# A short list of five slots after batch 3, GpSimd in one fixed order, and dilated values loaded ahead of plain queries

## The chip, the cores and the metric

The kernel runs on one core of a Trainium2 chip. The metric is the device time of one execution in microseconds (us); the time before is a median of 3 runs. A core has engines that run side by side, each in its own order of instructions: TensorE (PE, with its weight loads shown as PEld), VectorE (DVE), ScalarE (ACT), GpSimd (POOL) and SyncE (SP). SP only issues transfers here (16 DMA engines move them), and GpSimd issues some too: plain stores, scatters and gathers by index.

## What is computed

Two stages. The first is banded attention over 8 batches, 8 heads, 576 positions and 64 channels: heads 0 to 3 ("plain") see the last 32 positions, heads 4 to 7 ("dilated") every fourth of the last 128. The second is a mixture of 8 experts with one expert to a token, over the 8 x 576 = 4608 rows of 512 channels that attention gives.

```python
rel = pos[:, None] - pos[None, :]
mask_plain = (rel >= 0) & (rel < window)                                        # window = 32
mask_dil = (rel >= 0) & (rel < window * dilation) & (rel % dilation == 0)       # dilation = 4
...
logits = x @ w_gate + modality_bias[modality_id]
e_idx = np.argmax(logits, axis=1)
...
for e in range(E):
    mask = e_idx == e
    ...
    h = np.maximum(x[mask] @ w1[e], 0.0)
    out[mask] = gate_w[mask, None] * (h @ w2[e])
```

The weights of one expert are 512x1024 and 1024x512 floats, 4 MB together. The bias of the modality (spread 0.5) outweighs the rest of the logits, so that nearly all tokens go to few experts. Counted with the reference for its inputs at seed 0, all 4608 tokens split into 1621, 2290 and 697 for experts 1, 6 and 7; those of batches 0 to 3 into 821, 1114 and 369, those of batches 0 to 4 into 1047, 1396 and 437.

## The kernel before, in words

**Units and steps.** Attention goes by units: a batch has nine, `m` = 0 to 8 (L676 to L680): four of plain heads, one mixed (`m` = 4), four of dilated heads, 128 score rows each. The main loop (L942) makes one step `t` for each of the 72 units and overlaps them: step `t` emits the scores of unit `t` (matmuls L340, mask L343, maximum L346, and the subtraction on GpSimd, L347), the exponent of unit `t`-1 on ACT (L351), the transposed probabilities of `t`-2 (L356, L359), the product with the values of `t`-3 (L365, L380), the transposed output of `t`-4 (L387 to L392) with its store to `x_dram` by GpSimd (L402), and the gate's logits of `t`-5 (L411).

**Order.** PE, DVE, ACT and SP run in the order of the program's text (`MANUAL`, L20, L920). GpSimd isn't in that set: calls through `pool` (class `InOrder`, L269) pass `keep_in_program_order` and leave their name in `state['pool']`; the scatters into `table` (L497) are held behind that one instruction, and nothing else ties the calls to each other. L274, the line in `InOrder`, is the profile's line for all of them.

**Loads.** SP issues all loads of a batch in program order: `k` and `q` come in tiles `st` of four heads (L116, 4 transfers of 144 KB), plain values `vw` in one transfer (L127), dilated values in twelve of 16 to 64 KB (L131). For the batch after, dilated `k` is issued at the end of step `m`=1, dilated `q` at `m`=2, plain values at the start of `m`=3; for the batch after that, plain `k` at the end of `m`=6 and plain `q` at `m`=7; the first six transfers of the next batch's dilated values come at the end of `m`=8, and the other six at the start of `m`=0. ACT copies a shifted edge of the values at the end of steps `m` = 0 to 2 (plain) and 4 to 6 (dilated) (`shift_v`, L137). `qk_chunks` turns `k` and `q` on PE in six chunks (L306), two in a step: the next batch's plain ones in `m` = 4 to 6, k first, then q, its dilated ones in `m` = 8, 0 and 1.

**Routing.** Five steps after the last unit of a batch, a task `background` (L719) is made; `advance` runs one piece of each task, twice in a step. `gating` finds each token's expert, rank and weight and scatters (row, weight, number) into `table`, 96 tokens at a time. After the batch named in `EARLY` (batch 4), `slot_info` makes a short list of the full slots of 256 tokens that can be served at once, here three; `fetch_slot` loads the rows' numbers of a slot (`idt`, L626, SP), `gather` fetches the rows (`xr`, four gathers by GpSimd, each followed by two pieces' pause, into one buffer), writes them to `x_slot` (L645, SP) and reads them back as `xg` (L651, SP). After batch 7 the same `slot_info` makes the list of all other slots, in 39 instructions of DVE or so.

**Slots.** There are 19 slots of one expert each: 18 of 256 tokens and a last one of 128. Each is eight rounds `f` of 12 matmuls 128x256 (L858), ReLU and split on ACT and DVE (L864, L865), and 6 matmuls 128x512 (L838); the weights are split into a high and a low part for each slot (L806, L807), two rounds ahead. An expert's 4 MB are loaded only where a slot's expert differs from the one before (L657 to L669). `slots` is a generator (`moe`), started at step 71 (`go` at L755), that the main loop advances between attention's steps by `step`, and after them `while not state['routed']` by one piece for two pieces of the routing (L1017 to L1020).

Of the kernel before, what the change touches and what calls it, by code (L numbers as in the profile page):

```python
# [22 lines left out]
B, H, S, D = 8, 8, 576, 64  # L23
# [12 lines left out]
GB = 96  # L36
NGB = S // GB
SLOT = 256
EARLY = ((4, 3),)
NEARLY = sum(n for _, n in EARLY)  # L40
NSTAT = 18 - NEARLY
NIDS = 6
# [22 lines left out]
def kernel(  # L65
# [73 lines left out]
    state = {('qk', 0, 0): load_qk(0, 0, nc.scalar)}  # L139
# [129 lines left out]
    class InOrder:  # L269


        def __getattr__(self, name):
            def issue(*args, **kw):
                ins = tc.keep_in_program_order(getattr(nc.gpsimd, name)(*args, **kw))  # L274
                state['pool'] = ins.ins
                return ins
            return issue

    pool = InOrder()
# [439 lines left out]
    def background(b):  # L719


        if b < B - 1:
            yield
        steps = gating(b, state['lT', b])
        if b in round_of:
            for _ in steps:
                yield
                if ('counts', b) in state:
                    break
            yield from together(steps, slot_info(state['counts', b], round_of[b]))  # L730
            if round_of[b] > 0:
                return
            yield
            for n in range(2):
                fetch_slot(n)
                yield
            for _ in gather(0, ids_of[0]):
                yield
                yield

            while state['t'] < (B - 1) * 9:
                yield
            for _ in range(3):
                load_more(0, 1)
                yield
                yield
            steps = prepare_x(0, ids_of[0])
            for i in range(6):
                if i % 2 == 0:
                    load_more(0, 1)  # L750
                next(steps, None)
                yield
            while state['t'] < NU - 2:
                yield
            state['go'] = True  # L755
            return
        yield from steps
        if b == B - 1:
            yield
            yield from slot_info(state['counts', b], len(EARLY))  # L760
            yield from rest_info()
            state['routed'] = True

    def run(*pieces):
        for p in pieces:
            for _ in p:
                pass

    def together(*pieces):

        pieces = list(pieces)
        while pieces:
            for p in list(pieces):
                if next(p, pieces) is pieces:
                    pieces.remove(p)
            yield
# [150 lines left out]
    def step(share=MOE_RATE / 6):  # L927

        nonlocal credit
        if moe:  # L930
            credit += share if state['t'] < NU else 1
            while credit >= 1:
                credit -= 1
                next(moe, None)
# [7 lines left out]
    for t in range(NU + LAG + 1):  # L942
# [5 lines left out]
            psum['o'] = ctx.enter_context(tc.tile_pool(name="ps_o1", bufs=1, space=PSUM))  # L948
            moe = slots(NS, ids_of, ahead, hold)
        b, m = t // 9, t % 9  # L950
        if t == 1:
            pieces = qk_chunks(1, *state['qk', 0, 1])
        if t < NU:
            jobs = order[t][1]
            if m == 0:
                state['lT', b] = gwk.tile([2 * NE, S], F32, name="lT")
            if b + 1 < B:
                if m == 4:
                    pieces = qk_chunks(0, *state['qk', b + 1, 0])
                elif m == 8:  # L960
                    pieces = qk_chunks(1, *state['qk', b + 1, 1])
            if m == 0 and b > 0:
                load_v(b, 1, slice(6, None))
            elif m == 3:
                if b + 1 < B:
                    state['v', b + 1, 0] = load_v(b + 1, 0)
            units.append(Unit(b, m, jobs, [state['v', b, 0], state['v', b, 1]] if m >= 4 else [state['v', b, 0]], state['lT', b]))
            units[t].scores()
# [21 lines left out]
            units[t - 4].store()  # L990
            units[t - 4].keep(pool)

        for h in {0: (0,), 1: (1,), 2: (2, 3)}.get(m, ()) if 2 < t < NU else {0: (0, 1), 1: (2, 3)}.get(t, ()):
            shift_v(b, 0, h)
        for h in {4: (0,), 5: (1,), 6: (2, 3)}.get(m, ()) if t < NU else ():
            shift_v(b, 1, h)
        for i in range(2):
            step()
            if i < len(pieces):
                pieces[i]()  # L1000
        pieces = pieces[2:]
        if t < NU and b + 1 < B:

            if m == 1:
                state['k', 1] = load_one(b + 1, 1, k)
            elif m == 2:
                state['qk', b + 1, 1] = load_one(b + 1, 1, q), state['k', 1]
            elif m == 6 and b + 2 < B:
                state['k', 0] = load_one(b + 2, 0, k)
            elif m == 7 and b + 2 < B:  # L1010
                state['qk', b + 2, 0] = load_one(b + 2, 0, q), state['k', 0]
            elif m == 8:
                state['v', b + 1, 1] = load_v(b + 1, 1, slice(0, 6))
        advance([*round_of, B - 1] if moe and t < NU else range(-1, B))


    while not state['routed']:  # L1017
        step(1)
        advance()
        advance()  # L1020
    run(moe)
    man.close()
# [34 lines left out]
```

## Time and profile before

| what | value |
|---|---|
| time before, median of 3 runs | 711.53 us (710.65 to 712.71) |
| profiled execution, its own time | 710.85 us |
| span of the profile (first to last instruction) | 709.1 us |
| mean granted clock of TensorE | 0.959 |
| PE busy | 649.3 us (92%) |
| DVE, ACT, POOL busy | 497.4, 437.9, 290.0 us |
| moved by DMA | 94.95 MB, 134 GB/s |
| SP's queue (q1) | 146612 packets, 63.89 MB |

How to read it: times in the views are us from the span's start. A row of the timeline has start, length, engine, line, operation, what it writes and reads, and in brackets how long the engine had been idle and who ended that. A row of a table by stretches gives the stretch, its length, each engine's busy time with its number of instructions, the granted TensorE clock (1.00 is full, 0.50 half), the DMA engines' busy share and GB/s. SP's rows are issues, not landings.

### The profile page before, as it was taken

Reading aid. Unit: us, or ns where it says so; the run is one execution under the profiler, and the core shown is the slowest. Engines: PE = TensorE matmul, PEld = TensorE weight load, DVE = VectorE, ACT = ScalarE, POOL = GpSimd, SP = SyncE. Lnnn points to the kernel's source line nnn. Section 1 sums busy time; section 2 is a strip of 40 time slices with the busy share of each in tenths; the row PEclk is TensorE's granted clock in tenths of the full one; section 3 lists DMA queues with packets and bytes.
Section 4 is the critical chain, followed back from the end, with each engine's and each line's share of the span. In section 5 each row is a group of like instructions: output and inputs, shape, how many; then the busy total and the mean of one; then the engine's idle time right before and its main releaser. Section 6 shows DMA issues by size and latency. Waiting matters only on the chain. (4 is left out here: it accounts for less than half of the span.)

```text
span 709.1 us, 17888 instructions
## 1 busy us (share of the span) xinstructions
PE 649.3 (92%) x6286; PEld 571.1 (81%) x6286; DVE 497.4 (70%) x1212; ACT 437.9 (62%) x964; POOL 290.0 (41%) x396
## 2 busy tenths in 40 slices
PE   6799998997887899799999999999999999999991
PEld 3688787786776688689999999999999999999980
DVE  1688886886876778677766776667766677667660
ACT  3587896886766656355665565565666556655650
POOL 7345774865668553533333232233313231310110
PEclk7799999999899699999999999999999999999996
DMA  9898698697976943213433972333222346821730
GB/s 159 144 233 180 150 193 169 150 195 145 166 167 159 257 131 77 61 61 91 138 131 78 263 185 79 74 114 106 96 83 82 99 120 182 219 74 46 203 86 13
DMA packets 163233, 94.95 MB, mean 134 GB/s; under 512 B 124144, under 2 KB 143090, under 8 KB 163140
## 3 DMA queue, kind: packets, MB, share of 16 engines
q1 hardware_dynamic: 146612, 63.89, 40.3%
q0 software_dynamic: 11120, 28.64, 13.4%
q10 hardware_dynamic: 5408, 1.24, 1.0%
q8 instruction: 51, 0.84, 0.6%
q14 instruction: 42, 0.34, 0.2%
HBM read 127.52 MB, written 29.39 MB: 221 GB/s over the span
## 5 line engine op out<-in xcount | busy, mean ns | idle before, releaser
L858 PE MATMUL pt<-xh,w1l 128*128 128x256 f32 (+1 forms) x608 | 172.9, 284 | 7.7 <-DVE w1l L807 7.7
L858 PE MATMUL pt<-xl,w1h 128*128 128x256 f32 (+1 forms) x608 | 172.3, 283 | 0.0
L858 PE MATMUL pt<-xh,w1h 128*128 128x256 f32 (+1 forms) x608 | 172.2, 283 | 0.0
L864 ACT ACTIVATE hh<-pt 128x256 fp32r<-128x256 f32 (+1 forms) x152 | 57.6, 379 | 159.5 <-PE pt L858 159.4
L807 DVE TENSOR_TENSOR w2l<-w2q,w2h 128x512 fp32r<-128x512 f32 x152 | 104.9, 690 | 43.0 <-ACT w2h L806 34.7
L274 POOL DMA_INDIRECT xr<-x_dram,idt x74 | 82.5, 1115 | 120.4 <-DMA x_slot<-xr 72.2
L858 PEld LDWEIGHTS pt<-xh,w1l 128*128 128x128 f32 x608 | 116.7, 192 | 8.6 <-DVE w1l L807 8.5
L858 PEld LDWEIGHTS pt<-xh,w1h 128*128 128x128 f32 x608 | 116.5, 192 | 6.8 <-ACT w1h L806 0.2
L858 PEld LDWEIGHTS pt<-xl,w1h 128*128 128x128 f32 x608 | 116.6, 192 | 5.7
L838 PE MATMUL py<-w2h,hh 128*128 128x512 f32 x296 | 118.1, 399 | 0.0
L838 PE MATMUL py<-w2h,hl 128*128 128x512 f32 x296 | 117.1, 396 | 0.0
L838 PE MATMUL py<-w2l,hh 128*128 128x512 f32 x296 | 116.1, 392 | 0.0
L865 DVE SCALAR_TENSOR_TENSOR hl<-pt,hh 128x256 fp32r<-128x256 f32 (+1 forms) x152 | 63.3, 416 | 73.9 <-ACT hh L864 73.8
L274 POOL DMA_INDIRECT out_dram<-ys,idt x37 | 39.6, 1071 | 179.4 <-ACT ys L841 115.8
L807 DVE TENSOR_TENSOR w1l<-w1q,w1h 128x512 fp32r<-128x512 f32 x152 | 104.1, 685 | 2.7 <-ACT w1h L806 2.7
L806 ACT CAST w1h<-w1q 128x512 fp32r<-128x512 f32 x152 | 94.4, 622 | 3.3 <-DMA w1q<-in_moe_w_dram 3.3
L806 ACT CAST w2h<-w2q 128x512 fp32r<-128x512 f32 x152 | 93.1, 612 | 0.0
L274 POOL TENSOR_TENSOR sm<-sm,nmx 128x384 f32<-128x384 f32 x72 | 59.8, 830 | 61.9 <-DVE den L372 45.5
L365 PE MATMUL po<-vw,pT 96*64 96x65 f32 x1152 | 57.0, 238 | 11.3 <-ACT pT L359 6.7
L359 ACT COPY pT<-pt 96x512 f32<-96x512 f32 x72 | 41.5, 576 | 41.3 <-PE pt L356 40.2
L838 PEld LDWEIGHTS py<-w2l,hh 128*128 128x128 f32 x296 | 55.8, 189 | 13.2
L365 PEld LDWEIGHTS po<-vw,pT 96*64 96x64 f32 x1152 | 44.5, 145 | 24.6 <-ACT pT L359 11.4
(160 smaller groups left out, 1110.7 us busy)
## 6 DMA issues: line engine op xcount, KB each, us to landing
w2q<-in_moe_w_dram SPq DMA_DIRECT2D x76, 512.0 KB
w1q<-in_moe_w_dram SPq DMA_DIRECT2D x152, 256.0 KB
st<-in_k_dram SPq DMA_DIRECT2D x64, 144.0 KB
x_slot<-xr SPq DMA_DIRECT2D x18, 512.0 KB
xg<-x_slot SPq DMA_DIRECT2D x72, 128.0 KB
x_dram<-x_sb POOLq DMA_DIRECT2D x32, 256.0 KB, 3.6
st<-in_q_dram SPq DMA_DIRECT2D x56, 144.0 KB
vw<-in_v_dram SPq DMA_DIRECT2D x8, 576.0 KB
```

The lines of the kernel that those rows point to most:

```text
L274: ins = tc.keep_in_program_order(getattr(nc.gpsimd, name)(*args, **kw))
L359: nc.scalar.copy(out=self.pT, in_=src)
L365: nc.tensor.matmul(out=pov[u * TQ:(u + 1) * TQ, h, :], lhsT=self.pT[:, h, u * TQ:(u + 1) * TQ], rhs=self.vts[kd][:, h, i, :], start=True, ...
L806: nc.scalar.copy(out=hi, in_=raw)
L807: nc.vector.tensor_tensor(out=lo, in0=raw, in1=hi.bitcast(F32), op=ALU.subtract)
L838: nc.tensor.matmul(out=py[u], lhsT=ht[:, us], rhs=wt, start=(f + n == 0), stop=(f + n == FC + 1))
L858: nc.tensor.matmul(out=ph, lhsT=wt[:, c, :], rhs=xt[:, c, 0:cols], start=(c + i == 0), stop=(c + i == KC + 1))
L864: nc.scalar.activation(out=hh, in_=ph, func=AF.Relu)
L865: nc.vector.scalar_tensor_tensor(out=hl, in0=ph, scalar=0.0, in1=hh.bitcast(F32), op0=ALU.max, op1=ALU.subtract)
```

## The change

It does five things. The short list is made after batch 3 and has five slots instead of three; its pieces come at half the pace (`spaced`). The gathers of slot 0 come one a step from step 48 on at the earliest, those of slot 1 one a step from step 57 on, before the slots' generator starts, which finds slot 1's rows under way (`fetching`, `todo['rows'] = 2`). Each call through `pool` is placed behind the one before it. The dilated values of the next batch are issued at the ends of `m`=7 and `m`=8, and plain queries after them, at the end of `m`=0; at the kernel's start the turning of dilated q and k and the edge copies move by a step. After the last step the routing gets one piece for three pieces of the slots, not two for one.

```diff
-EARLY = ((4, 3),)
+EARLY = ((3, 5),)
...
                 ins = tc.keep_in_program_order(getattr(nc.gpsimd, name)(*args, **kw))
+                if 'pool' in state:
+                    tc.add_manual_dep(ins.ins, state['pool'].name, mybir.DependencyInfo(mybir.DependencyClass.NoSync, mybir.DependencyReason.SCHED_ONLY),
+                                      reason="GpSimd's order")
                 state['pool'] = ins.ins
...
-            yield from together(steps, slot_info(state['counts', b], round_of[b]))
+            yield from together(steps, spaced(slot_info(state['counts', b], round_of[b])))
...
-            for _ in gather(0, ids_of[0]):
-                yield
-                yield
+
+            for n, t0 in ((0, (b + 1) * 9 + 12), (1, (b + 2) * 9 + 12)):
+                rows = gather(n, ids_of[n])
+                while state['t'] < t0:
+                    yield
+                for _ in range(4):
+                    next(rows)
+                    yield
+                    yield
+                if n == 0:
+                    for _ in rows:
+                        yield
+            fetching.append((1, rows))
+            todo['rows'] = 2
...
+    def spaced(piece):
+
+        for _ in piece:
+            yield
+            yield
...
-        if t == 1:
+        if t == 2:
             pieces = qk_chunks(1, *state['qk', 0, 1])
...
-            if m == 0 and b > 0:
-                load_v(b, 1, slice(6, None))
-            elif m == 3:
+            if m == 3:
...
-        for h in {0: (0,), 1: (1,), 2: (2, 3)}.get(m, ()) if 2 < t < NU else {0: (0, 1), 1: (2, 3)}.get(t, ()):
+        for h in {0: (0,), 1: (1,), 2: (2, 3)}.get(m, ()) if 2 < t < NU else {1: (0, 1), 2: (2, 3)}.get(t, ()):
             shift_v(b, 0, h)
...
-        for i in range(2):
-            step()
+        at_once = 3 if t < 4 else 2
+        for i in range(at_once):
+            if i < 2:
+                step()
             if i < len(pieces):
                 pieces[i]()
-        pieces = pieces[2:]
+        pieces = pieces[at_once:]
...
-            elif m == 7 and b + 2 < B:
-                state['qk', b + 2, 0] = load_one(b + 2, 0, q), state['k', 0]
+            elif m == 7:
+                state['v', b + 1, 1] = load_v(b + 1, 1, slice(0, 6))
             elif m == 8:
-                state['v', b + 1, 1] = load_v(b + 1, 1, slice(0, 6))
+                load_v(b + 1, 1, slice(6, None))
+            elif m == 0 and b > 0:
+                state['qk', b + 1, 0] = load_one(b + 1, 0, q), state['k', 0]
...
     while not state['routed']:
-        step(1)
-        advance()
+        for _ in range(3):
+            step(1)
         advance()
```

## The prediction

> **What bounds the kernel now.** I read the page first, then tables by stretches, then waits, then timelines of single engines. The page's first line and a table of engines by stretch give the frame. The first seven stretches are the batches 1 to 7; the eighth is the first two slots with attention's last units among them; the last is the other 17 slots.
>
> ```profile
> span 709.1 us, 17888 instructions
> ...
> core 0: us, PE busy (x) PEld busy (x) DVE busy (x) ACT busy (x) POOL busy (x), PEclk, DMA share, GB/s
> 44.20:70.60 26.40, 24.75 (x445) 21.24 (x443) 22.40 (x75) 22.19 (x55) 13.48 (x24) 1.00 0.85 188
> 70.60:97.10 26.50, 24.91 (x445) 21.30 (x443) 22.60 (x75) 22.12 (x55) 19.01 (x30) 1.00 0.80 169
> 97.10:127.10 30.00, 26.49 (x446) 22.59 (x443) 22.70 (x76) 22.32 (x55) 18.99 (x30) 0.94 0.88 174
> 127.10:154.10 27.00, 25.10 (x445) 21.25 (x443) 22.53 (x75) 22.11 (x55) 18.89 (x30) 1.00 0.85 175
> 154.10:185.70 31.60, 26.85 (x453) 22.85 (x450) 23.10 (x79) 22.28 (x55) 19.00 (x30) 0.95 0.87 163
> 185.70:217.80 32.10, 27.46 (x446) 22.98 (x443) 25.68 (x93) 22.55 (x55) 22.51 (x33) 0.95 0.66 149
> 217.80:252.20 34.40, 28.01 (x406) 23.20 (x405) 24.72 (x79) 21.19 (x51) 23.17 (x33) 0.75 0.90 220
> 252.20:312.10 59.90, 52.55 (x393) 46.38 (x391) 46.26 (x134) 30.11 (x66) 29.11 (x30) 0.97 0.27 73
> 312.10:693.30 381.20, 380.76 (x2438) 344.82 (x2436) 267.19 (x470) 228.31 (x473) 101.61 (x92) 1.00 0.42 120
> ```
>
> I set the stretches so that each batch holds its 9 units x 16 = 144 score matmuls; the same table for line 340 alone shows it for the last:
>
> ```profile
> 217.80:252.20 34.40, 6.26 (x144) 4.25 (x144) 0.75 0.90 220
> ```
>
> Batches 1 and 2 take 26.4 and 26.5 us (mean 26.45) at full clock, with PE, DVE and ACT all above 80% busy: that is the pace where nothing waits. Batches 3 to 7 are over it by 3.5, 0.5, 5.1, 5.6 and 7.9 us, 22.6 together. In the 17 slots PE is never free (380.8 of 381.2 us); nothing there can be won by order. One slot, from a stretch of exactly eight rounds, is the first row here; the others are the stretches in which the clock was halved, and one with an expert's load in it:
>
> ```profile
> 334.80:357.35 22.55, 22.55 (x145) 20.46 (x144) 16.02 (x29) 13.60 (x29) 6.89 (x6) 1.00 0.37 118
> 117.92:121.33 3.41, 3.41 (x37) 3.07 (x30) 2.73 (x9) 3.06 (x9) 0.82 (x1) 0.50 1.29 242
> 193.02:196.43 3.41, 3.41 (x39) 2.96 (x39) 2.67 (x10) 2.88 (x8) 2.45 (x4) 0.50 0.35 77
> 227.15:237.39 10.24, 9.40 (x105) 7.80 (x106) 7.09 (x19) 7.52 (x18) 8.72 (x10) 0.50 1.06 251
> 302.25:305.65 3.40, 3.11 (x12) 2.97 (x13) 3.22 (x9) 1.19 (x3) 0.00 (x0) 0.50 0.04 2
> 400.00:420.00 20.00, 20.00 (x129) 18.05 (x128) 13.56 (x26) 12.09 (x25) 6.64 (x7) 1.00 0.73 198
> ```
>
> Two slots are 45.1 us, so of the stretch of 59.9 us 14.8 are attention's tail and waits. The waits that ended before the halved stretches, in PE's and ACT's timelines and PE's waits from 292 to 303 us:
>
> ```profile
> 116.71 0.55 PE L306 MATMUL pt<-ident,st 96*128 96x96 f32 x4 [2.35 <-ACT kT L311]
> ...
> 173.60 0.62 ACT L137 COPY vw<-vw 32x520 f32<-32x520 f32 x1 [4.83 <-DMA st<-in_k_dram]
> ...
> 192.49 0.24 PE L411 MATMUL po<-uxl,wgs 128*16 128x128 f32 x1 [1.85 <-DVE uxl L392]
> ...
> 227.99 1.14 PE L365 MATMUL po<-vw,pT 96*64 96x65 f32 x16 [3.30 <-ACT pT L359]
> ...
> PE pt L858 <- DVE w1l L807: 6.3, 2, 5.2
> ```
>
> So: batches 3 and 5 wait for dilated values (ACT stands at the edge copy; the releaser's name is the queue's, the tile copied is `vw`), batch 6 for DVE, batch 7 for the probabilities, the slots for the split weights.
>
> **The change, part by part.**
>
> *Dilated values ahead of plain queries.* SP's issues in batches 4 and 5, and PE where it meets the queries in unit (5, 4):
>
> ```profile
> 128.50 9.19 SPq L131 DMA_DIRECT2D vw<-in_v_dram  x12
> ...
> 152.40 4.07 SPq L116 DMA_DIRECT2D st<-in_q_dram  x4
> 156.57 14.14 SPq L131 DMA_DIRECT2D vw<-in_v_dram  x12
> ...
> 176.63 0.58 SPq L127 DMA_DIRECT2D vw<-in_v_dram  x1
> ...
> 161.89 0.56 PE L340 MATMUL pss<-kT,qT 64*64 64x96 f32 x16
> ...
> 168.21 0.49 PE L306 MATMUL po<-ident,st 96*128 96x96 f32 x4
> ...
> 169.20 0.56 PE L340 MATMUL pss<-kT,qT 64*64 64x96 f32 x16
> ```
>
> Queries took 4.07 us to issue, the twelve value transfers 14.14 (9.19 a batch before). Swapped, values come 4.07 us sooner, and ACT's 4.83 us of waiting fall to about 0.8. But the queries then end where the values ended, at 170.7, and PE wants them in the same step, at 168.21. Chunk 0 takes heads 0 and 1, the first two of four transfers, half of 4.07 or 2 us before the last; with about 2 us from issue to landing (170.7 to 173.6 was 2.9) PE would stand from 168.2 to about 171 or 172. It stood 3.27 us before, some instructions further on. The wait moves more than it goes. Batch 3 alike: PE's 2.35 us become about 2. I take -0.5 us for batches 3 and 4 together, between -3.5 (all of batch 3's excess) and +1. In batch 5 the short list's six scatters now run one every half step beside batch 4's end, not beside the values; if the transfers' 14.14 us fall towards 9.19, the queries come in time. I take a PE wait of 2 us there, not 4.
>
> *At the start*, dilated k and q are turned a step later. The plain queries of batch 1 come by the same loads as before, none of which the edit moves, and unit 5 stands behind them either way; what is won ahead of them is waited away. 0 us, at worst a halved window more, 1.7.
>
> *List after batch 3, gathers spread, GpSimd in order.* GpSimd from 199 to 230 us, SP's load of row numbers, and PE's largest wait from 200 to 213:
>
> ```profile
> 201.53 0.39 SPq L626 DMA_DIRECT2D idt<-table  x1
> ...
> 204.83 1.09 POOL L274 DMA_INDIRECT xr<-x_dram,idt  x1 [3.81 <-DMA idt<-table]
> ...
> 222.34 1.08 POOL L274 DMA_INDIRECT xr<-x_dram,idt  x1 [0.30 <-DVE uxl L392]
> 223.72 1.02 POOL L274 DMA_INDIRECT xr<-x_dram,idt  x1 [0.30 <-DVE den L373]
> 225.05 1.00 POOL L274 DMA_INDIRECT xr<-x_dram,idt  x1 [0.30 <-issue]
> 226.07 0.84 POOL L274 TENSOR_TENSOR sm<-sm,nmx 128x384 f32<-128x384 f32 x1
> ...
> PE po L365 <- ACT pT L359: 0.8, 1, 0.8
> ```
>
> At 222 us three gathers of slot 1 run in a row ahead of unit 65's subtraction; in the program's text they come only after step 71. That is batch 7's wait of 3.30 us, after which the clock was halved for 10.24 us. With the order fixed and these gathers at steps 57 to 60, one a step, both should go. Batch 7 goes from 34.4 to 28: -6.5 us. Not all 7.9, since it carries slot 0's preparation; between -7.9 and -3 (if the clock stays low for other reasons).
>
> Batch 6 loses the list's instructions (93 against 75 of DVE: 18, and 3.1 us more busy than in batch 2), PE's 1.85 us with a halved window behind it, slot 0's gathers and their 3.81 us for row numbers. It gets slot 1's four gathers (about 1.05 us and 0.3 idle each, 5.4 us of GpSimd, which is busy 22.5 of 32.1), and SP's write and read-back of slot 0. Slot 1's first gather needs the one buffer that this write empties, and the write stands behind batch 7's plain queries. -3 us, between -5.6 and 0.
>
> Batch 5 gets the list, at half pace, and slot 0's gathers. Here is the price. The row numbers are issued in step 49, behind the plain values of batch 6; those were due at step 48 (161.89) and were issued at 176.63, for SP runs 14.7 us behind its text in the full batches. The numbers would go out near 177.5, and from issue to gather it took 3.3 us in the row above (201.53 to 204.83) with little ahead of them; behind 576 KB some 2 more. The gather can run at 181 to 183, and stands on GpSimd right after unit 50's subtraction, at 169.2 + 2 (the queries) + 3 (my estimate from the scores to the end of the subtraction): 174 or so. GpSimd then waits 7 to 9 us, and the next subtraction behind it. A wait of 3.81 us cost PE 0.8 at most, so PE pays about 8 - 3.8 = 4 us, and 1.7 for a halved window. Batch 5: 26.45 + 2 + 4 + 1.7 less what overlaps, against 31.6; I say 33.6, +2 us, between -5 (row numbers early enough, no wait for queries) and +7.
>
> *Routing spread over the slots.* DVE from 294 to 301.25:
>
> ```profile
> 294.00:301.25 7.25, 6.42 (x40) 1.00 0.04 2
> ```
>
> The list of the other slots, 37 small instructions, fills DVE in one block while PE waits 6.3 us for split weights; then 3.4 us at half clock, of which half is lost: 8.0 us. After the change one piece comes for three of the slots' pieces: 11 pieces over 33, at four to a round eight rounds of 22.55/8 = 2.8 us. A slot leaves DVE 22.55 - 16.0 = 6.5 us idle and the splits run two rounds ahead, so about 6 us of list fit. Five slots, 113 us, cover it instead of three. -7.5 us, between -8 and -3.
>
> *Two more loads of an expert.* Full slots after batch 3, from the reference: 3 + 4 + 1 = 8, so five exist: three of expert 1 and two of expert 6; then 1 and 6 come again, two loads of 4 MB more. From 400 to 420 us such a load ran at 198 GB/s and PE was busy 20.00 of 20. A load takes 21 us of a slot's 22.55: 0 us, at worst +2.
>
> Sum: -0.5 + 2 - 3 - 6.5 - 7.5 = -15.5 us. The profiled execution took 710.85, 0.7 below the median of 711.53, so 696.0 against the median.
>
> **A rule of the clock.** Waits of 2.35 and 1.85 us were each followed by 3.41 us at 0.50 in the rows above, so I charge a halved window (1.7 us where PE is full) even to short waits. [...]
>
> **The rivals.**
>
> *Waits stay hidden.* SP catches up with the values moved (scatters out of their way): batch 5 ends 4 us under before and batch 6 5 us: -23.5, 688 us. For it: batch 6's wait of 3.81 us cost almost nothing. Against: SP's 14.7 us. 15%.
>
> *Attention wins nothing.* It is held by SP's queue, and what batch 7 gains, batches 5 and 6 lose; only routing's 7.5 remain: 704 us. 17%.
>
> *Slower: GpSimd in order becomes the bound.* A gather that waits for a transfer now holds every later subtraction and routing step. The waits of gathers on slot writes in all of before:
>
> ```profile
> POOL xr L274 <- DMA x_slot<-xr: 72.2, 14, 12.2
> ```
>
> If row numbers take 10 us and the buffer of slots 1 and 2 the longest, 12.2, each above a cover of 3.8: 6.2 + 8.4 + 8.4 = 23 us, with three halved windows 28, of which 5.7 are in my sum: +22, 718 us. It decides from GpSimd waits of about 27 us in all. For it: the order is strict and SP late; against: two gathers have a step between. 9%.
>
> [...] 4%.
>
> *It does not do what it says*, or gains and waits cancel: an empty slot in the list would cost 22.55 us, which the counts exclude; 711 us, 5%.
>
> **How the numbers follow.** My forecast has the other 50%, with its own range of 690 to 702. The range of 686 to 707 takes in most of the first two rivals and leaves out the slower one and the null: about 2 in 10. Faster is 50 + 15 + 17 + 4 = 86%, the same (within 0.3%, 2 us, about what a measurement of this kernel can tell) 5%, slower 9%.
>
> **What would show it.** In the profile after: batch 7 without three gathers in a row and PE without the 3.30 us; no block on DVE and no 5 us wait for `w1l` in the first slots; in batches 3 and 5 PE waiting at `st` (L306's line) for queries in place of ACT at `vw`; a gather in batch 5 with 7 to 9 us of idle time before it, released by `idt`. I am wrong if GpSimd's waits reach PE in the slots, if the last 17 slots show PE idle, or if batches 5 and 6 together take less than 58 or more than 67 us.

## The result and the profile after

The kernel after took 719.82 us (median of 4 runs, 716.37 to 724.02) against 712.12 us (4 runs, 710.65 to 715.17) for the kernel before: a ratio of 1.0102, 95% interval 1.0067 to 1.0136. It is slower, by 1%, where 15.5 us less were forecast. In a second set of runs it was 710.01 us (10 runs) against 706.36 (25 runs), 1.0044 (1.0019 to 1.0069): slower again, by less.

The profiled execution took 717.73 us. Line numbers of the kernel after are 3 above those of before up to the loads (L672), and 20 above them in the slots. First the page's line and the table of engines by stretch, cut at the same work as in the prediction: batches 1 to 7, slots 0 and 1, slots 2 to 18.

```profile
span 715.9 us, 17862 instructions
...
core 0: us, PE busy (x) PEld busy (x) DVE busy (x) ACT busy (x) POOL busy (x), PEclk, DMA share, GB/s
44.00:70.50 26.50, 24.86 (x448) 21.28 (x447) 22.51 (x75) 22.32 (x56) 13.57 (x24) 1.00 0.80 185
70.50:96.90 26.40, 24.85 (x444) 21.21 (x444) 22.58 (x76) 22.28 (x55) 18.97 (x30) 1.00 0.78 167
96.90:126.10 29.20, 26.28 (x444) 22.39 (x443) 22.86 (x76) 22.35 (x55) 18.91 (x30) 0.94 0.81 166
126.10:159.90 33.80, 28.23 (x452) 24.01 (x450) 23.24 (x79) 22.46 (x55) 18.96 (x30) 0.90 0.81 163
159.90:195.30 35.40, 27.52 (x445) 23.06 (x443) 26.55 (x94) 22.73 (x55) 21.49 (x33) 0.90 0.73 151
195.30:227.00 31.70, 25.41 (x445) 21.37 (x443) 24.87 (x81) 23.36 (x57) 27.99 (x39) 1.00 0.91 176
227.00:256.70 29.70, 25.83 (x407) 21.25 (x405) 23.34 (x73) 20.43 (x48) 15.34 (x25) 0.83 0.82 186
256.70:308.70 52.00, 50.88 (x391) 44.96 (x391) 40.49 (x104) 30.24 (x65) 28.39 (x28) 1.00 0.37 107
308.70:699.90 391.20, 384.17 (x2437) 345.74 (x2435) 271.42 (x501) 228.09 (x472) 109.32 (x95) 1.00 0.50 137
```

Two stretches are shorter than before: batch 7 (29.7 for 34.4) and slots 0 and 1 (52.0 for 59.9 us). Batch 4 grew by 6.8, batch 5 by 3.8. The last row has 10.0 us more than before, and PE is no longer busy in all of it: 384.2 of 391.2 us, against 380.8 of 381.2. PE's largest waits, over the whole span, say at what it stood:

```profile
PE po L309 <- DMA st<-in_q_dram: 11.1, 5, 4.2
PE po L475 <- DVE oh L466: 7.7, 7, 4.6
PE pt L878 <- ACT w1h L826: 5.4, 4, 2.5
```

The columns are us in total, times and longest. The first is the wait for plain queries (1.4 us in the kernel before), the second that for the gating, most of it in batch 5, and the third is in the slots, for ACT's split of expert weights. ACT in turn waits for their load, in its own waits of before and of after:

```profile
ACT w1h L806 <- DMA w1q<-in_moe_w_dram: 3.3, 2, 1.8
```

```profile
ACT w1h L826 <- DMA w1q<-in_moe_w_dram: 15.1, 4, 5.0
```

**Batches 4 and 5.** PE's timeline, at one place in each:

```profile
144.53 0.52 PE L309 MATMUL po<-ident,st 96*128 96x96 f32 x4 [4.25 <-DMA st<-in_q_dram]
...
187.95 0.27 PE L475 MATMUL po<-oh,upper 96*96 96x48 bf16 x1 [4.62 <-DVE oh L466]
```

Behind the second stand GpSimd and SP; their timelines (GpSimd's rows first, then SP's, then one of DVE's):

```profile
179.72 0.82 POOL L274 TENSOR_TENSOR sm<-sm,nmx 128x384 f32<-128x384 f32 x1 [2.21 <-DVE den L375]
185.96 1.10 POOL L274 DMA_INDIRECT xr<-x_dram,idt  x1 [5.41 <-DMA idt<-table]
187.09 0.29 POOL L274 TENSOR_TENSOR t<-t,ewt 96x48 f32<-96x48 f32 x1
...
177.59 1.54 SPq L127 DMA_DIRECT2D vw<-in_v_dram  x1
180.52 3.26 SPq L629 DMA_DIRECT2D idt<-table  x2
...
187.42 0.23 DVE L464 TENSOR_REDUCE m<-t 96x6 f32<-96x48 f32 x1 [4.17 <-POOL t L274]
```

Slot 0's first gather stood 5.41 us at the row numbers, which SP issued from 180.5 on. The gating's `t` came only at 187.09, behind the gather; DVE stood 4.17 us at it, and `oh` (DVE, 187.69) and PE's L475 follow from it. GpSimd began `t` 0.03 us after the gather's end.

**The slots.** GpSimd and SP ahead of slot 15, which loads an expert and starts at 610.6:

```profile
586.30 1.45 POOL L274 DMA_INDIRECT xr<-x_dram,idt  x1 [6.85 <-DMA x_slot<-xr]
588.06 1.31 POOL L274 DMA_INDIRECT xr<-x_dram,idt  x1 [0.30 <-issue]
594.18 1.03 POOL L274 DMA_INDIRECT out_dram<-ys,idt  x1 [4.81 <-ACT ys L861]
597.72 1.13 POOL L274 DMA_INDIRECT out_dram<-ys,idt  x1 [2.51 <-ACT w1h L826]
599.15 1.55 POOL L274 DMA_INDIRECT xr<-x_dram,idt  x1 [0.30 <-issue]
601.00 1.01 POOL L274 DMA_INDIRECT xr<-x_dram,idt  x1 [0.31 <-issue]
...
607.88 0.39 SPq L648 DMA_DIRECT2D x_slot<-xr  x1
...
611.00 1.81 SPq L654 DMA_DIRECT2D xg<-x_slot  x4
613.15 2.19 SPq L669 DMA_DIRECT2D w1q<-in_moe_w_dram  x4
```

A slot's four gathers come two ahead of two output scatters and two behind them; the scatters wait for results (4.81 and 2.51 us). So the rows of the slot (`x_slot`) go out 19.8 us after the running slot's start (588.1), and the second half of `w1`, behind them on SP, 2.5 us after slot 15 has begun. In the kernel before the four gathers of slot 15 stand in a row, ahead of the scatters; `x_slot` goes out 12.3 us after the running slot's start at 583.1, and this half of `w1` 0.8 us after slot 15's at 605.7. GpSimd's and SP's rows of before:

```profile
576.73 1.05 POOL L274 DMA_INDIRECT xr<-x_dram,idt  x1 [5.38 <-DMA x_slot<-xr]
578.09 1.32 POOL L274 DMA_INDIRECT xr<-x_dram,idt  x1 [0.31 <-issue]
579.71 1.00 POOL L274 DMA_INDIRECT xr<-x_dram,idt  x1 [0.30 <-issue]
581.02 1.19 POOL L274 DMA_INDIRECT xr<-x_dram,idt  x1 [0.30 <-issue]
589.24 1.03 POOL L274 DMA_INDIRECT out_dram<-ys,idt  x1 [7.03 <-ACT ys L841]
...
595.43 0.39 SPq L645 DMA_DIRECT2D x_slot<-xr  x1
...
606.49 2.19 SPq L666 DMA_DIRECT2D w1q<-in_moe_w_dram  x4
```

### The profile page after: what moved, and what is told of

The parts are those of the page before. It is cut to its first block, busy times and chain, and to the rows that moved or that the text cites. A ratio compares the mean times of both kernels' runs of the same rounds, so it can differ in the third digit from the quotient of the medians.

```text
span 715.9 us, 17862 instructions
## 1 busy us (share of the span) xinstructions
PE 650.7 (91%) x6286; PEld 570.5 (80%) x6286; DVE 498.3 (70%) x1212; ACT 438.6 (61%) x964; POOL 297.2 (42%) x396
## 2 busy tenths in 40 slices
DMA packets 167713, 103.34 MB, mean 144 GB/s; under 512 B 124528, under 2 KB 143474, under 8 KB 167620
## 5 line engine op out<-in xcount | busy, mean ns | idle before, releaser
L878 PE MATMUL pt<-xh,w1h 128*128 128x256 f32 (+1 forms) x608 | 172.5, 284 | 5.4 <-ACT w1h L826 5.4
L878 PE MATMUL pt<-xh,w1l 128*128 128x256 f32 (+1 forms) x608 | 172.8, 284 | 2.3 <-DVE w1l L827 2.3
L878 PE MATMUL pt<-xl,w1h 128*128 128x256 f32 (+1 forms) x608 | 172.2, 283 | 0.4 <-DVE xl L817 0.4
L274 POOL DMA_INDIRECT xr<-x_dram,idt x74 | 85.8, 1159 | 124.8 <-DMA x_slot<-xr 102.7
L827 DVE TENSOR_TENSOR w2l<-w2q,w2h 128x512 fp32r<-128x512 f32 x152 | 104.9, 690 | 41.1 <-ACT w2h L826 33.6
L878 PEld LDWEIGHTS pt<-xh,w1h 128*128 128x128 f32 x608 | 116.4, 191 | 13.8 <-ACT w1h L826 7.5
L878 PEld LDWEIGHTS pt<-xl,w1h 128*128 128x128 f32 x608 | 116.4, 192 | 6.2 <-DVE xl L817 0.7
L878 PEld LDWEIGHTS pt<-xh,w1l 128*128 128x128 f32 x608 | 116.6, 192 | 3.6 <-DVE w1l L827 3.5
L885 DVE SCALAR_TENSOR_TENSOR hl<-pt,hh 128x256 fp32r<-128x256 f32 (+1 forms) x152 | 63.1, 415 | 70.4 <-ACT hh L884 70.4
L274 POOL TENSOR_TENSOR sm<-sm,nmx 128x384 f32<-128x384 f32 x72 | 59.9, 832 | 69.0 <-DVE den L375 46.8
L362 ACT COPY pT<-pt 96x512 f32<-96x512 f32 x72 | 41.5, 577 | 51.8 <-PE pt L359 50.8
L858 PEld LDWEIGHTS py<-w2l,hh 128*128 128x128 f32 x296 | 55.8, 188 | 13.2
L368 PE MATMUL po<-vw,pT 96*64 96x65 f32 x1152 | 56.3, 237 | 8.6 <-ACT pT L362 3.7
L858 PEld LDWEIGHTS py<-w2h,hh 128*128 128x128 f32 x296 | 56.3, 190 | 6.7
```

The source lines that it names most:

```text
L362: nc.scalar.copy(out=self.pT, in_=src)
L368: nc.tensor.matmul(out=pov[u * TQ:(u + 1) * TQ, h, :], lhsT=self.pT[:, h, u * TQ:(u + 1) * TQ], rhs=self.vts[kd][:, h, i, :], start=True, ...
L827: nc.vector.tensor_tensor(out=lo, in0=raw, in1=hi.bitcast(F32), op=ALU.subtract)
L858: nc.tensor.matmul(out=py[u], lhsT=ht[:, us], rhs=wt, start=(f + n == 0), stop=(f + n == FC + 1))
L878: nc.tensor.matmul(out=ph, lhsT=wt[:, c, :], rhs=xt[:, c, 0:cols], start=(c + i == 0), stop=(c + i == KC + 1))
L885: nc.vector.scalar_tensor_tensor(out=hl, in0=ph, scalar=0.0, in1=hh.bitcast(F32), op0=ALU.max, op1=ALU.subtract)
```

## The experiments

The theories. *Order*: the fixed order puts gathers behind scatters that wait for results, so a slot's rows and the weights behind them on SP come late. *Loads*: the two further loads of an expert cost the slots their time. *Queue*: the queries, now last in SP's queue, make PE wait in batches 3 and 4, and the row numbers, late on SP, hold GpSimd and the gating in batch 5. *List*: batch 5 is long by the list's own work, earlier than before.

The kernels ran in four groups and not all on one chip; each ratio is to runs of the kernel before made on the same chip with its group. The stages in us come from one profile of each. The same kernel's batches 3 and 4 differ by some us from one execution to another (after: 29.2 and 33.8, again 32.7 and 27.8), so small differences of one stage are not read.

| kernel | batches 3+4 | 5 | 6+7 | slots 0, 1 | slots 2 to 18 | ratio (95%) |
|---|---|---|---|---|---|---|
| before | 57.0 | 31.6 | 66.5 | 60.0 | 378.9 | |
| before, again | 55.6 | 27.1 | 65.6 | 61.7 | 378.7 | |
| after | 63.1 | 35.4 | 61.4 | 52.0 | 389.2 | 1.0102 (1.0067 to 1.0136) |
| after, again | 60.5 | 38.6 | 56.1 | 51.8 | 389.4 | 1.0044 (1.0019 to 1.0069) |
| 1 after, free order | 56.6 | 37.3 | 60.2 | 51.9 | 381.7 | 0.9989 (0.9956 to 1.0022) |
| 2 after, queries first | 55.3 | 37.7 | 56.4 | 51.8 | 392.7 | 1.0020 (0.9985 to 1.0054) |
| 3 after, three slots | 57.0 | 36.8 | 55.8 | 51.8 | 393.5 | 1.0092 (1.0056 to 1.0128) |
| 4 before, two more loads | 56.2 | 27.1 | 68.2 | 60.1 | 384.8 | 1.0057 (1.0022 to 1.0092) |
| 5 after, fixed until routed | 59.4 | 34.6 | 58.0 | 53.4 | 385.9 | 1.0000 (0.9969 to 1.0030) |
| 6 before, values first | 56.1 | 27.1 | 66.7 | 61.0 | 378.9 | 1.0039 (1.0006 to 1.0072) |
| 7 after, gathers of slot 0 later | 60.4 | 29.7 | 67.8 | 50.9 | 396.5 | 1.0136 (1.0094 to 1.0177) |
| 8 before, list after batch 3 | 53.2 | 35.2 | 57.2 | 63.7 | 379.1 | 1.0034 (0.9996 to 1.0073) |
| 9 before, fixed order | 55.1 | 28.9 | 62.9 | 62.8 | 384.5 | 1.0102 (1.0022 to 1.0182) |
| 10 before, four slots, routing spread | 56.3 | 29.7 | 64.1 | 51.9 | 379.4 | 0.9849 (0.9776 to 0.9923) |
| the same, again | 57.2 | 28.3 | 64.5 | 52.1 | 379.4 | 0.9897 (0.9867 to 0.9927) |
| 11 after, both gathers later | 58.9 | 29.6 | 63.8 | 49.7 | 380.8 | 0.9974 (0.9946 to 1.0001) |
| 12 before, five slots, routing spread | 54.6 | 33.6 | 61.1 | 53.1 | 380.1 | 0.9885 (0.9858 to 0.9913) |

**1. After, GpSimd's order free.**

```diff
-                if 'pool' in state:
-                    tc.add_manual_dep(ins.ins, state['pool'].name, ...)
```

> The changed kernel without the fixed order of GpSimd (the three added lines in InOrder are out); all else as changed. Order theory: in the slots the fixed order splits a slot's gathers around the output scatters, the slot's write and the weights behind it on SP come late, and that costs the 10.3 us more of slots 2 to 18. Then those slots fall from 389 to 379-381 us, the PE waits on w1h (5.4 us) go, and the time is 708-711 us. Loads theory: the two further loads of an expert cost it, whatever GpSimd does: slots 2 to 18 stay at 387-390, the time at 716-721. In both, GpSimd may move gathers ahead again in batch 7, which gives back up to 5 us.

705.30 us; slots 2 to 18 fell to 381.7. GpSimd and SP ahead of slot 15, which here starts at 597.4:

```profile
567.96 1.05 POOL L274 DMA_INDIRECT xr<-x_dram,idt  x1 [4.86 <-DMA x_slot<-xr]
569.31 1.25 POOL L274 DMA_INDIRECT xr<-x_dram,idt  x1 [0.31 <-issue]
570.87 1.00 POOL L274 DMA_INDIRECT xr<-x_dram,idt  x1 [0.30 <-issue]
572.17 1.20 POOL L274 DMA_INDIRECT xr<-x_dram,idt  x1 [0.30 <-issue]
581.00 1.03 POOL L274 DMA_INDIRECT out_dram<-ys,idt  x1 [7.63 <-ACT ys L858]
...
587.19 0.39 SPq L645 DMA_DIRECT2D x_slot<-xr  x1
...
596.26 1.81 SPq L651 DMA_DIRECT2D xg<-x_slot  x4
598.42 2.19 SPq L666 DMA_DIRECT2D w1q<-in_moe_w_dram  x4
```

All four gathers precede the scatters, and `w1`'s second half goes out 1.0 us into slot 15 in place of 2.5. The order costs some 7.5 us in the slots. The 2.8 us that stay above before (about 1 us each in slots 3, 5 and 15) this run doesn't explain. Runs 11 and 12 below load experts in the same slots with GpSimd's order free there, and their slots 5 and 15 take 22.6 us, so these loads alone don't cost it.

**2. After, queries ahead of values as before.**

```diff
-            elif m == 7:
-                state['v', b + 1, 1] = load_v(b + 1, 1, slice(0, 6))
+            elif m == 7 and b + 2 < B:
+                state['qk', b + 2, 0] = load_one(b + 2, 0, q), state['k', 0]
...
```

> The changed kernel with the loads of the main loop in the old order (plain queries at m=7, dilated values at m=8 and m=0); the start, the list of five, the fixed order and the spread routing stay. Queue theory: batch 4 lost 6.8 us because the queries now end the chain of SP's loads and the values run among the scatters: batch 4 falls from 33.8 to 27-28 us, the PE waits for st in L309 at unit 40 and unit 62 go, and the time is 711-714. DVE theory: batches 4 and 5 lost to the list's small instructions on DVE and the earlier scatters: batch 4 stays above 32, the time at 717-721.

709.61 us. Batches 3 and 4 are at 55.3 in place of 60.5 and 63.1, but batch 5 stays at 37.7: its cost isn't the load order's. The slots kept theirs (392.7), as they should with the order fixed.

**3. After, with three slots in the list after batch 3,** so that no expert is loaded twice more.

```diff
-EARLY = ((3, 5),)
+EARLY = ((3, 3),)
```

> The changed kernel with a list of three slots after batch 3 in place of five: the first three slots are of expert 1, and expert 1 goes on, so that the two further loads of an expert do not exist (4 loads as before). Loads theory: slots 2 to 18 fall from 389 to 379-381 us, the time to about 709-711. Order theory: the loads that are left (slots 6, 15, 18) still cost 1.5 to 2 us each, slots 2 to 18 take 382-386 us, the time is 712-716. Attention stays as changed (batch 4 near 33.8, batch 5 near 35.3).

713.86 us. The further loads are gone (94.95 MB moved, 103.34 in the kernel after), and the slots are no shorter: 393.5. Of these 7.7 us are one wait in slot 2, since three slots are too short a cover for the spread list:

```profile
PE pt L878 <- ACT xh L816: 7.7, 1, 7.7
```

Behind it slot 3 ran partly at half clock (24.7 us for 22.6; the page has 8 tenths of the clock in the slice from 319 to 337 us). Without both some 384 are left, 5 above before, and these stand in the two loads that the kernel before has too (slots 6 and 15 took 25.4 and 24.5 us for 22.6). So the further loads are not needed for a loss: loads that were free before now cost.

**4. Before, with two loads more,** by loading in slots 3 and 5 whether the expert changes or not.

```diff
-            loads_of[n] = [fetch_weights(si_of[n], n == 0), 0]
+            loads_of[n] = [fetch_weights(si_of[n], n in (0, 3, 5)), 0]
```

> The kernel before, with the weights of slots 3 and 5 loaded without condition (the same bytes once more): two further loads of 4 MB and nothing else. Order theory: PE stays full in the slots as at slots 6 and 15; within 2 us of before, 711-714. Loads theory: a load right after attention or two loads close together cost what the changed kernel lost at slots 3 and 5, 4.7 and 1.6 us: 717-719.

710.84 us; slots 2 to 18 at 384.8, 6 above before. But slot 6, right behind the forced load of slot 5, took 4.1 of it (26.7 us), and the lone loads of slots 3 and 5 0.5 each. Two loads back to back are an accident of my choice of slots, which the kernel after doesn't have; the run settles less than it was meant to.

**5. After, order fixed only until the other slots' list is made,** beside before and after on one chip.

```diff
-                if 'pool' in state:
+                if 'pool' in state and not state.get('routed'):
```

> The kernel before, unchanged, for its stages on the chip of the three kernels beside it. Every theory expects the batches of its first profile within 1 us each (26.5, 26.5, 30.0, 27.1, 31.6, 32.0, 34.4), about 60 us for slots 0 and 1, 379 us for slots 2 to 18 and about 711 us in all. If the batches differ by more than 1 us here, single batches are not to be compared across chips.

> The kernel after, unchanged. Every theory expects 0.7 to 1.4% above the kernel before on the same chip, slots 0 and 1 near 52 us and slots 2 to 18 near 389 us, with the surplus of 10 us in the slots that load an expert. What it settles is whether batch 4's 33.8 and batch 5's 35.4 us come again; in the runs on another chip batch 4 was 29 to 30 us with the same order of loads.

> The kernel after, with GpSimd's order fixed only until the list of the other slots is made. The order theory (a fixed order holds the gathers back between output scatters, so a slot's table and the weights behind it on SP come late) expects slots 2 to 18 at 381 to 383 us and attention as in the kernel after on this chip: about 7 us less than it, 0.990 of it. The loads theory (the two further loads cost PE by themselves) expects slots 2 to 18 to stay at 389 us and no gain. If instead the fixed order was what held attention up, the total falls by as much as with no fixed order at all, with shorter batches 3 to 5.

706.72 us against 710.01 of the kernel after. Slots 5, 8 and 15 fell from 24.1 to 24.4 us to 22.6; slot 3, one of whose gathers was still behind two scatters, took 29.0, with one wait of PE for `w1h` of 3.51 us and 6.83 us at half clock about it, where the matmuls of L878 started every 0.21 us in place of 0.12. So 385.9 instead of the 381 to 383 expected: three of the four slots did what the order theory says, the fourth did not. The two controls also show how far single batches go between executions: before's batch 4 was 27.1 and 29.2, which missed the bound of 1 us that I had set.

**6. Before, values ahead of queries.**

```diff
-            if m == 0 and b > 0:
-                load_v(b, 1, slice(6, None))
-            elif m == 3:
+            if m == 3:
...
+            elif m == 0 and b > 0:
+                state['qk', b + 1, 0] = load_one(b + 1, 0, q), state['k', 0]
```

> The kernel before, with only the order of loads changed in the units: dilated values one unit sooner and plain queries last. The queue theory (queries now last among SP's transfers, values among the scatters) expects batches 3 and 4 together to lose 0 to 6 us, PE waiting for st in L306 in place of ACT at the values, and batches 5 to 7 unchanged within 2 us: 711 to 718 us, 1.000 to 1.010. My prediction's term says -0.5 for batches 3 and 4 and about +2 for batch 5. The list theory (batch 5's length comes from the earlier list, not from the queue) expects batch 5 to stay within 1 us of before, well under 35 us.

707.36 us, 0.4% slower. Batches 3 and 4 took 56.1 (55.6 before on this chip), with PE now waiting 1.75 us from 138.4 on for queries; batch 5 stayed at 27.1. By itself the swap gains nothing. Over all profiles, batches 3 and 4 took 56.1 to 63.1 us with values first (8 profiles, mean 59.0) and 53.2 to 57.2 with queries first (9, mean 55.6). That difference isn't the swap's alone: seven of the eight have other parts of the change as well.

**7. After, slot 0's gathers four units later.**

```diff
-            for n, t0 in ((0, (b + 1) * 9 + 12), (1, (b + 2) * 9 + 12)):
+            for n, t0 in ((0, (b + 1) * 9 + 16), (1, (b + 2) * 9 + 12)):
```

> The kernel after, with slot 0's gathers four units later (from step 52 in place of 48), so that the row numbers have landed when GpSimd comes to them. The queue theory (GpSimd stands at gather 0 for row numbers that SP issues late, the gating behind it stops, and PE with it) expects PE's wait of 4.6 to 7.1 us for oh to fall under 2 us, no halved window behind it, and batch 5 at 28 to 31 us in place of 34.6 to 38.6; the gathers in batch 6 cost up to 3 us there. In all 4 to 7 us under the kernel after: 0.995 to 1.000 of before. The list theory (the earlier list loads DVE in batch 5 by itself) expects batch 5 to stay above 34 us.

715.90 us, 1.0136 of before: no gain, a miss in the total. Batch 5 did what the queue theory said (29.7 us). Batch 6 gave it all back; the rows of batches 5 and 6, and GpSimd in batch 6:

```profile
157.80:187.40 29.60, 25.57 (x444) 21.34 (x443) 26.33 (x93) 22.89 (x57) 19.33 (x30) 1.00 0.78 171
187.40:226.50 39.10, 33.34 (x443) 28.63 (x443) 24.38 (x80) 22.08 (x54) 28.09 (x38) 0.74 0.82 181
```

```profile
202.34 0.83 POOL L274 TENSOR_TENSOR sm<-sm,nmx 128x384 f32<-128x384 f32 x1
209.73 1.05 POOL L274 DMA_INDIRECT xr<-x_dram,idt  x1 [6.56 <-DMA x_slot<-xr]
```

Slot 1's gather now stands at the one gather buffer, whose write SP issued at 203.69. PE waited 2.74 us at 212 and its clock was 0.74 over the batch. Slots 2 to 18, with the same order on GpSimd as in the kernel after, took 7 us more than there. In this profile, of the slowest execution of the ten (722.48 us), PE's waits for `w1h` were 3.42, 2.25 and 1.42 us, each with halved clock about it, 17.1 us in all; in the kernel after, the halved clock came to 3.4 us in these slots. At a granted clock of 0.50 half of the time counts as lost; by this estimate (17.1 - 3.4)/2 = 6.9 us, most of the 7. Why the waits were longer isn't known.

**8. Before, with only the list moved.**

```diff
-EARLY = ((4, 3),)
+EARLY = ((3, 5),)
```

> The kernel before, with the list after batch 3 with five slots and nothing else: GpSimd's order free, queries ahead of values, gathers of slot 0 right behind the list, routing of the other slots in one block. The order theory expects slots 2 to 18 at 379 to 382 us although two more experts are loaded; the loads theory 386 to 389. The queue theory expects batch 5 at 33 to 38 us by the wait for row numbers behind SP's lag, as in the kernel after, and batches 6 and 7 some 3 us each shorter than before. In all 0.995 to 1.010 of before; slots 0 and 1 near 60 us.

708.32 us. The slots' row beside that of run 9:

```profile
308.20:687.30 379.10, 378.58 (x2429) 343.07 (x2428) 265.91 (x468) 227.34 (x470) 100.33 (x92) 1.00 0.52 141
```

Two more experts are loaded (141 GB/s against 120), and PE is free for 0.5 us of 379.1: these further loads cost nothing while the order is free. Batch 5 took 35.2, with a gather's wait of 4.3 us for row numbers.

**9. Before, with only the order fixed.**

```diff
+                if 'pool' in state:
+                    tc.add_manual_dep(ins.ins, state['pool'].name, ...)
```

> The kernel before with GpSimd's order fixed and nothing else. The order theory expects slots 2 to 18 some 3 to 7 us longer than 378.7 to 378.9 by itself, most in the slots that load an expert (6, 15, 18), since the fixed order stands the gathers behind the output scatters: 1.004 to 1.010 of before if attention stays. My prediction expects batch 7 to lose its wait of 3.3 us and the halved windows behind it (34 to about 29 us), for the three gathers then stand behind unit 65's subtraction: 0.992 to 0.997. Both can be so at once; the stages tell them apart.

```profile
306.70:691.20 384.50, 380.70 (x2429) 344.32 (x2428) 266.21 (x468) 227.32 (x470) 103.98 (x92) 1.00 0.41 119
```

712.73 us, 1.0102. The slots grew by 5.8 us, nearly all in the two that load an expert (slot 6: 26.8, slot 15: 24.1), without one load more. Batch 7 took 31.6 us in place of 33.9: its wait of 3.3 us for the probabilities went, and one of 3.26 us for `uxl` came later in the batch.

**10. Before, four slots in the list after batch 4, routing spread.**

```diff
-EARLY = ((4, 3),)
+EARLY = ((4, 4),)
...
-        step(1)
-        advance()
+        for _ in range(3):
+            step(1)
```

> The kernel before with four slots in the list after batch 4 in place of three, and the list of the other slots spread three slot steps to a piece; GpSimd's order free, order of loads and gathers as before. My routing term (7.5 us, measured 7.9 to 9.9 in the kernel after) and no part that was found to cost: slots 0 and 1 at 52 us in place of 60 to 62, attention within 1.5 us of before, slots 2 to 18 at 379 to 382 if four slots cover the list. 0.988 to 0.993 of before. If four slots are too few, slot 3 stalls by up to 8 us, as slot 2 did with three, and nothing is won.

> The kernel before with four slots in the list after batch 4 and the other slots' list spread, a second time for a closer interval: 0.980 to 0.990 of before, from 9 us less in slots 0 and 1 and no other change. If the first figure was chance, 0.990 or more.

697.14 us, and 698.02 in the second run (before beside them: 706.31 and 705.55). The gain is in slots 0 and 1, 8 to 10 us, and nothing is given back.

**11. After, both sets of early gathers four units later, order fixed in attention's units only.**

```diff
-                if 'pool' in state:
+                if 'pool' in state and state.get('t', 0) < 72:
...
-            for n, t0 in ((0, (b + 1) * 9 + 12), (1, (b + 2) * 9 + 12)):
+            for n, t0 in ((0, (b + 1) * 9 + 16), (1, (b + 2) * 9 + 16)):
```

> The kernel after with both sets of early gathers four units later (slot 0's from step 52, slot 1's from step 61) and GpSimd's order fixed only within attention's units. With slot 0's gathers alone moved, slot 1's first gather stood 6.56 us at the one gather buffer, whose write to the slot SP had issued at 203.69, and batch 6 took 39.1 us. The theory that each such wait on GpSimd in order is what PE loses expects: no wait over 2 us of a gather for idt or x_slot in batches 5 and 6, batch 5 at 28 to 31, batch 6 at 28 to 32, slots 2 to 18 at 380 to 383 us, 0.985 to 0.993 of before. The rival, that these batches are long by the list's work itself and waits only show it, expects batches 5 and 6 together still above 66 us and 0.995 or more.

704.15 us, 0.9974: less than expected. The rows of batches 5 and 6:

```profile
156.20:185.80 29.60, 25.63 (x445) 21.38 (x443) 26.32 (x93) 22.98 (x57) 19.29 (x30) 1.00 0.79 160
185.80:215.50 29.70, 26.36 (x443) 22.24 (x443) 22.72 (x75) 22.44 (x56) 23.42 (x33) 0.94 0.94 197
```

No gather waits for row numbers any more, none in these batches for the buffer, and both batches take under 30 us with the list in the first of them. This decides between waits and work: the list costs batch 5 about 3 us (29.6 against 26.45), what went with the gathers' waits on GpSimd cost the other 5 to 9 (34.6 to 38.6 in runs with the early gathers in order). Batch 7, which took over slot 1's gathers, rose to 34.1 and so kept the total up. With the order free behind attention the slots took 380.8.

**12. Before, five slots after batch 3, routing spread;** none of the change's other parts.

```diff
-EARLY = ((4, 3),)
+EARLY = ((3, 5),)
...
-        step(1)
-        advance()
+        for _ in range(3):
+            step(1)
```

> The kernel before with the list of five slots after batch 3 and the list of the other slots spread, and without the change's other parts (GpSimd's order free, queries first, gathers of slot 0 behind the list, of slot 1 as before). The order theory expects attention as with the list alone (244.5 us to the first slot), slots 0 and 1 at 52, slots 2 to 18 at 379 to 382 although two more experts are loaded: 0.987 to 0.994 of before. If the loads need the fixed order's absence and routing's gain is eaten by the third early slot's wait, 0.997 or more.

698.28 us, 0.9885. As fast as run 10, with 8 MB more moved. These two are the fastest kernels of the study; their intervals overlap, so neither is shown to be the better.

## Why the prediction was wrong

The forecast was -15.5 us and the profile shows +6.8 in the span. The difference of 22.3 us, by its terms (us, from the starts of the stages, in the first pair of profiles):

| term | forecast | measured | off by |
|---|---|---|---|
| start and batches 1, 2 | 0 | -0.3 | -0.3 |
| batches 3 and 4 | -0.5 | +6.1 | +6.6 |
| batch 5 | +2 | +3.8 | +1.8 |
| batch 6 | -3 | -0.3 | +2.7 |
| batch 7 | -6.5 | -4.7 | +1.8 |
| routing (slots 0 and 1) | -7.5 | -8.0 | -0.5 |
| slots 2 to 18 | 0 | +10.3 | +10.3 |

*The step that failed* is "nothing there can be won by order": from PE being busy in 380.8 of 381.2 us it was concluded that order could not matter in the last 17 slots, and they were charged only with the loads, at "0 us, at worst +2". Nothing could be won, but something could be lost. I followed the fixed order through batches 5 to 7 and not through the slots, where the same helper issues gathers and scatters. Only the prediction's last lines look there: they name PE idle in the last 17 slots as a sign of being wrong, and PE was idle there for 7.0 us. (Their sign for batches 5 and 6, more than 67 us together, came too, barely: 67.1.) The slack could have been read: `w1`'s second half was issued 0.8 us after slot 15's start in the kernel before, so little was left to give when the rows ahead of it came 7.5 us later. Runs 1, 5 and 11 show the order as the cause by taking it out of the slots, run 9 by adding it alone (5.8 us). The loads alone cost nothing (run 8). The two together cost more than the order alone: in the kernel after each of the slots 3, 5, 8 and 15, which load an expert, took 1.5 to 4.7 us more than 22.6. So the "0 us" for the loads, read from a row with the order free, held only there.

*Batches 3 and 4.* That the wait moves from values to queries was right; that it moves at no cost was not, in the kernel after. PE stood 4.25 us at the queries of unit 40 and the clock was halved behind it, for 6.83 us. The swap alone, on the kernel before, cost these batches 0.5 us (run 6), inside the term's range; in the kernel after, where they took 60.5 and 63.1 us, taking it out brought 55.3 (run 2). So the term was too small for the swap among the other parts; which of them adds to the queries' wait stays open, and single profiles differ by some us.

*Batch 5.* The gather's wait came in the step and by the cause named (5.41 us in the first profile, 7.9 in the second, "7 to 9" forecast). PE paid 4.62 and 7.09 for the 4 forecast: the wait reaches PE through the gating rather than through the subtraction. That the sum came near is in part luck: the 2 us at queries did not come (0 and 0.84), the list's own 3 us (run 11) were not in it, and 6.83 us ran at half clock for the 3.41 charged. Batch 5 grew by 3.8 and, in the second pair of profiles, 11.5 us; the latter lies above the term's +7. Runs 7 and 11 show most of it as the gather's.

*Batches 6 and 7* were right in sign. In the second pair they lost 9.5 us together, as forecast; in the first only 5.

*Routing* was right: 8.0 and 9.9 us, and it is the one part found to pay, with a list of four or five slots to cover it (runs 10 and 12). *The start* was right. The excess of batches 3 to 7 that the prediction puts at 22.6 us is 22.9 by its own table; nothing hangs on it.

*The rival that ends slower* gave 718 us, near the 717.73 of the profile, but not for its reason. It priced gathers held by row numbers and by the buffer within attention. The first was in my sum already; the second did not come within attention of the kernel after, and came there, with 6.56 us, only in run 7. What decided stood in the slots, where no rival looked: that 718 comes near is luck. *The charge for short waits* was right in kind: in the kernel after, waits of 4.25, 2.93 and 2.55 us were followed by 6.83, 3.41 and 3.41 us at 0.50, one of 1.43 us was not (below).

*Left open*: why PE's waits in the slots of run 7 were longer, what holds 2.8 us in those of run 1, and why batch 4 or 3 is the long one in different executions. The earlier gathers of slot 1 and the edits at the kernel's start were not run alone.

## What to carry to other kernels

Where an engine's order is fixed, follow every instruction that the same queue carries to the end of the program, not only through the stretch that the edit was made for: here gathers stood behind scatters that waited 4.81 and 2.51 us for their results. An engine that is busy all the time in a stretch tells that nothing can be won there, and nothing of how much can be lost (PE was busy 380.8 of 381.2 us in the slots, and they grew by 10.0); read from the issue times how late the last input comes that is still early enough. When a bundle of edits is slow, run each part on the kernel before alone: here the spread routing list, with four or five early slots to cover it, was worth 7 to 9 us on the kernel before, and was lost in the bundle.

## What the runs showed of the hardware

In the 17 profiles, between 60 and 650 us, PE at full clock stood 0.9 us or longer 127 times. A stretch at 0.50 began within 3.5 us of the wait's end after 38 of 38 waits of 2.25 us or more, 9 of 16 from 1.8 to 2.25, 18 of 34 from 1.3 to 1.8, and 5 of 39 below that. Sixteen more stretches at 0.50 had no wait above 0.7 us in the 7 us ahead of them. Their lengths are 3.41, 6.83, 10.24 and 13.65 us, whole multiples of 3.41. In the profiles of before and after alone, where PE stood 0.9 us or longer 17 times, a stretch began 0.2 to 1.3 us behind the end of six waits (1.85 to 4.25 us), before the end of four others (1.75, 3.30, 4.62 and 5.22 us) and at none of the seven of 0.95 to 1.43 us.

In each profile the starts and ends of these stretches lie on one grid of 3.41 us, to within 2 ns (in the kernel after the starts 107.48, 145.03, 185.99 and 226.94 lie 11, 12 and 12 steps apart). Counted in the steps of that grid from 60 to 640 us that ran at full clock: of 44 with PE busy for less than half, 43 had half clock in the next step; of 166 from 0.50 to 0.75, 47; of 2538 above that, none. In before and after alone it was 9 of 9, 3 of 19 and none of 291. The ends of matmuls, and so the shares, are modelled. What sets the clock was not shown.
